# Batch 0 of an attention-and-FFN kernel: blocks of 128, 256 and 384 query rows against two blocks of 384

## Chip, cores and metric

The kernel runs on one core of a Trainium2 chip. The metric is the device time of one execution in microseconds (us). Five engines work beside each other: PE (matmuls; its weight loads are shown as PEld), DVE (elementwise, reads PSUM), ACT (activations, reads PSUM), POOL and SP. SP and POOL also issue DMAs.

## What is computed

```python
# B, H, S, D = 4, 8, 768, 64; 16 centroids a head
q_assign = argmax(q_n @ c_n.T); k_assign = argmax(k_n @ c_n.T)   # per head
mask = q_assign[:, :, :, None] == k_assign[:, :, None, :]
scores = where(mask, q @ k.T / 8, -1e9)
attn = softmax(scores) @ v                       # (B, H, S, D)
x = attn.transpose(0, 2, 1, 3).reshape(3072, 512)
out = (sigmoid(x @ w_gate) * (x @ w_val)) @ w_out   # 512 -> 1536 -> 512
```

Each query sees only the keys that fall to the same centroid. An FFN with a sigmoid gate follows.

## The kernel before

Heads go in pairs (4 pairs a batch), keys in 6 chunks of 128, queries in blocks of n x 128 rows. The work on a pair has two halves.

**Preparing a pair.** q and k are loaded by SP in fp32 (load_side, load_pair, L73 to L84), split into a high and a low fp16 part (split_h L189 on DVE or ACT, split_l L197 on DVE), and transposed: for batches 0 and part of 1 by PE (trans_pe L211, evac L222), later by DMA (trans_dma L230). PE then multiplies with the centroids (logits L237, 24 small matmuls a side), and DVE takes the maximum and compares (onehot L251). The one-hot rows, scaled, become 16 more rows of the transposed q and k, so that the score matmul itself adds a large constant where the clusters agree. They get there in two ways: rows (L274) transposes on PE, copies on DVE and sends them with small DMAs of 24 KB from SP; rows_pad (L292), used for k of batch 0 and q of its pair 0, transposes them padded, so that one copy by DVE or ACT from PSUM puts them in place.

**Attention** (att, L436). For each pair and key chunk: two score matmuls (L490), one exp over both heads on ACT (L499), and, behind it, 2 x n AV matmuls (L450), one exp behind for n = 1 and two for more. At the end of a pair DVE adds the mean term of v and takes the reciprocal (L460, L469), and Pool (DVE for n = 1) multiplies (L470). v is cast by prep_v (L361, one pair at a time, Pool or ACT), and its sum over keys comes from mean_v: for batch 0 by 24 matmuls on the casts, for later batches by Pool's sum_v and a single matmul a half batch.

**FFN** (ffn_in L520, ffn_out L546). 96 matmuls for n x 128 rows with tanh on ACT (L540) and a product on DVE (L542), then 12 matmuls of 512 columns (L552) for each 128 rows. The FFN of one block is cut into single matmuls, which ffn_some hands out between the steps of the next block's attention.

**Batch 0** runs in blocks of 128, 256 and 384 queries, every other batch in two of 384 (BLK, L565). For the first block the rows 0, 6, 12 ... of q are loaded for all heads in one tile (qn0, L93), and have a path of their own (q0_split, q0_trans, q0_classify, q0_rows; T0), so that only k must be prepared in full for it (first_block, L622). The other queries of batch 0 are prepared during the first two blocks. xT, the transposed input of the FFN, comes for the first two blocks from PE transposes (x_trans, L422), else from a DMA transpose (L511).

The order of work is written by hand in the lead-in and from the middle of the third block on. Between, PE, DVE and ACT are left to a scheduler, while SP and POOL keep the program's order; an instruction that depends on nothing can still come to stand earlier than the program has it, among the instructions of the lead-in. at (L573) lists what is to be issued at which half step. Three PSUM banks ("f") serve everything but scores and AV.

Of the kernel before, what the change touches and what calls it, by code (L numbers as in the profile page):

```python
# [20 lines left out]
def kernel(  # L21
# [18 lines left out]
    MCH = 3  # L40
    MB = MCH * 128
    NFC = FF // 128
    NDC = DM // 128
    es_scale = 1.0 / (D ** 0.5 * SC * SC)
# [15 lines left out]
    hp = ctx.enter_context(tc.tile_pool(name="h", bufs=1))  # L60
# [12 lines left out]
    def load_side(b, pr, side):  # L73
        t = NAT[b, pr, side] = natp.tile([128, 2, NCH, D], FP, name="nat")
        nc.sync.dma_start(
            out=t,
            in_=(q, k)[side][b, 2 * pr : 2 * pr + 2].rearrange(
                "h (p c) d -> p h c d", c=NCH
            ),
        )  # L80

    def load_pair(b, pr):
        load_side(b, pr, 1)
        load_side(b, pr, 0)  # L84

    def load_v(b, g):
# [5 lines left out]

    qn0 = natp.tile([128, H, D], FP, name="nat")  # L93
    nc.sync.dma_start(
        out=qn0, in_=q[0].rearrange("h (p c) d -> p h c d", c=NCH)[:, :, 0, :]
    )
    for pr in range(NPR):
        load_side(0, pr, 1)
    load_v(0, 0)
    load_v(0, 1)  # L100
    for pr in range(NPR):
        load_side(0, pr, 0)
# [24 lines left out]
    ohq0 = const.tile([128, H, D + NCL], HP)  # L127
    nc.gpsimd.memset(ohq0, 0.0)
    ohk0 = [const.tile([128, 2, NCH, D + NCL], HP, name=f"ohk0{i}") for i in range(2)]
    nc.gpsimd.memset(ohk0[0], 0.0)  # L130
    nc.gpsimd.memset(ohk0[1], 0.0)
# [119 lines left out]
    def onehot(b, pr, side):  # L251
        if b == 0 and (side == 1 or pr == 0):
            dst = ohk0[pr % 2][:, :, :, D : D + NCL]
        else:
            if side == 1 or b == 0:
                OH[b, pr] = ohp.tile([128, NCH, 2, 2, NCL], HP, name="ohw")
            dst = OH[b, pr][:, :, side, :, :].rearrange("p c h x -> p h c x")
        clv = CL[b, pr, side][:, 0 : 2 * NCH * NCL].rearrange("p (g x) -> p g x", x=NCL)
        mx = smp.tile([128, 2 * NCH], FP, name="mx")
        nc.vector.tensor_reduce(mx, clv, AX.X, ALU.max)  # L260
        nc.vector.tensor_tensor(
            dst,
            clv.rearrange("p (h c) x -> p h c x", h=2),
            mx.rearrange("p (h c) -> p h c", h=2)
            .unsqueeze(3)
            .to_broadcast([128, 2, NCH, NCL]),
            ALU.is_equal,
        )
# [5 lines left out]
    def rows(b, pr):  # L274
        ns = 1 if b == 0 else 2
        po = fp_.tile([32 * ns, 1024], HP, name="f")
        for c in range(NCH):
            nc.tensor.transpose(  # L278
                po[:, bass.ts(c, 128)],
                OH[b, pr][:, c, 0:ns, :, :].rearrange("p s h x -> p (s h x)"),  # L280
                ident,
            )
        ohc = ohp.tile([32 * ns, S], HP, name="ohc")
        nc.vector.tensor_scalar(ohc, po[:, 0:S], OHV, None, ALU.mult)
        for side in range(ns - 1, -1, -1):
# [6 lines left out]
    def rows_pad(pr, side, hh, eng=None):  # L292
        po = fp_.tile([128, 1024], HP, name="f")
        for c in range(NCH):
            nc.tensor.transpose(  # L295
                po[0 : D + NCL, bass.ts(c, 128)], ohk0[pr % 2][:, hh, c, :], ident
            )
        dst = T[0, pr, side][D : D + NCL, hh, :]
# [7 lines left out]
    hl0 = hlp.tile([128, H, 2, D], HP, name="hl")  # L306
    T0 = const.tile([128, H, 128], HP)

    def q0_split():
        nc.vector.tensor_scalar(hl0[:, :, 0, :], qn0, SC, None, ALU.mult)  # L310
        nc.vector.scalar_tensor_tensor(
            hl0[:, :, 1, :], qn0, SC, hl0[:, :, 0, :], ALU.mult, ALU.subtract
        )

    def q0_trans():
        pt = fp_.tile([128, 1024], HP, name="f")
        for h in range(H):
            nc.tensor.transpose(
                pt[:, bass.ts(h, 128)], hl0[:, h, :, :].rearrange("p a d -> p (a d)"), ident
            )  # L320
        nc.scalar.copy(T0.rearrange("p h n -> p (h n)"), pt)

    def q0_classify():
        cl = fp_.tile([128, 512], FP, name="f")
        for h in range(H):
            for r in range(2):
                nc.tensor.matmul(
                    out=cl[:, bass.ts(h, NCL)],
                    lhsT=T0[:, h, :],
                    rhs=cT[:, r, bass.ts(h, NCL)],  # L330
                    start=(r == 0),
                    stop=(r == 1),
                )
        clv = cl[:, 0 : H * NCL].rearrange("p (h x) -> p h x", x=NCL)
        mx = smp.tile([128, 2 * NCH], FP, name="mx")
        nc.vector.tensor_reduce(mx[:, 0:H], clv, AX.X, ALU.max)
        nc.vector.tensor_tensor(
            ohq0[:, :, D : D + NCL],
            clv,
            mx[:, 0:H].unsqueeze(2).to_broadcast([128, H, NCL]),  # L340
            ALU.is_equal,
        )

    def q0_rows():
        po = fp_.tile([128, 1024], HP, name="f")
        for h in range(H):
            nc.tensor.transpose(po[0 : D + NCL, bass.ts(h, 128)], ohq0[:, h, :], ident)
        nc.vector.tensor_scalar(
            T0[D : D + NCL, :, :].rearrange("p h n -> p (h n)"),
            po[D : D + NCL, :],  # L350
            OHV,
            None,
            ALU.mult,
        )


# [4 lines left out]
    def prep_v(b, pr, eng=None):  # L361

        va = VA[b, pr] = vap.tile([128, 2, NCH, D + 1], HP, name="va", bufs=2 * NPR)
        nc.gpsimd.memset(va[:, :, :, D : D + 1], 1.0)
        h = 2 * (pr % 2)
        src = VN[b, pr // 2][:, h : h + 2, :, :]
        if eng is nc.scalar:
            nc.scalar.copy(va[:, :, :, 0:D], src)
        else:
            nc.gpsimd.tensor_copy(va[:, :, :, 0:D], src)  # L370

    def sum_v(b, g):
        hs = bass.ts(g, H // 2)
        vn = VN[b, g]
        if g == 0:
            VS[b] = smp.tile([128, H, D + 1], HP, name="vs", bufs=1)
            nc.gpsimd.memset(VS[b][:, :, D : D + 1], float(NCH))
# [9 lines left out]
    def mean_v(b, hs):  # L387

        if b not in SV:
            SV[b] = vap.tile([128, H, D + 1], FP, name="sv")  # L390
        sp = fp_.tile([128, 512], FP, name="f")
        n = len(hs) * (D + 1)
        if b == 0:
            for c in range(NCH):
                nc.tensor.matmul(
                    out=sp[:, 0:n],
                    lhsT=ones,
                    rhs=VA[b, hs[0] // 2][:, :, c, :],
                    start=(c == 0),
                    stop=(c == NCH - 1),  # L400
                )
        else:
            nc.tensor.matmul(
                out=sp[:, 0:n],
                lhsT=ones,
                rhs=VS[b][:, hs[0] : hs[-1] + 1, :],
                start=True,
                stop=True,
            )
        nc.vector.tensor_scalar(  # L410
            SV[b][:, hs[0] : hs[-1] + 1, :].rearrange("p h d -> p (h d)"),
            sp[:, 0:n],
            EPS,
            None,
            ALU.mult,
# [3 lines left out]
    X = {}  # L419
    XT = {}  # L420

    def x_trans(b, c0, n, pr):  # L422

        if pr == 0:
            XT[b, c0] = xp.tile([128, MCH, NDC, 128], HP, name="xT")
        ps = fp_.tile([128, 1024], HP, name="f")
        for t in range(n):
            nc.tensor.transpose(
                ps[:, bass.ts(t, 128)], X[b, c0][:, t, bass.ts(pr, 128)], ident
            )  # L430
        nc.vector.tensor_copy(
            XT[b, c0][:, 0:n, pr, :],
            ps[:, 0 : n * 128].rearrange("p (t n) -> p t n", t=n),
        )

    def att(b, c0, n):  # L436
        x = X[b, c0] = xp.tile([128, MCH, DM], HP, name="x")
        pend = []
        G = 3 if n == 1 else 1
        avt = [None]  # L440

        def av_part(pr, j0, es):
            if j0 == 0:
                avt[0] = avp.tile([128, 512], FP, name="av")
            av = avt[0]
            for g in range(G):
                for hh in range(2):
                    for t in range(n):
                        o = (hh * n + t) * (D + 1)
                        nc.tensor.matmul(  # L450
                            out=av[:, o : o + D + 1],
                            lhsT=es[:, hh, bass.ts(g * n + t, 128)],
                            rhs=VA[b, pr][:, hh, j0 + g, :],
                            start=(j0 + g == 0 and hh == 0 and t == 0),
                            stop=(j0 + g == NCH - 1 and hh == 1 and t == n - 1),
                            skip_group_check=True,
                        )
            if j0 + G == NCH:
                s = smp.tile([128, 2, MCH, D + 1], FP, name="avs")
                nc.vector.tensor_tensor(  # L460
                    s[:, :, 0:n, :],
                    av[:, 0 : 2 * n * (D + 1)].rearrange("p (h t d) -> p h t d", h=2, t=n),
                    SV[b][:, 2 * pr : 2 * pr + 2, :]
                    .unsqueeze(2)
                    .to_broadcast([128, 2, n, D + 1]),
# [334 lines left out]
```

## Time and profile before

| | us |
|---|---|
| median of 3 runs (364.88 to 366.35) | 365.16 |
| the profiled execution | 365.16 |
| its span in the profile | 363.4 |
| first scores of batch 0, of its block of 256, of 384 | 15.1, 33.8, 62.2 |
| first scores of batch 1, 2, 3 | 91.9, 172.9, 255.2 |

The first scores are the first start of line L490 for each block; two score matmuls start at 15.1, and the ten that follow at 16.4. In the page, a group's line gives busy time and mean ns of one; "idle before" is the engine's idle time and what ended it. PEclk is the clock granted to PE. A view of busy times by stretch has the stretch, its length, then busy us and number of instructions of PE, PEld, DVE, ACT and POOL, the granted clock, the share of busy DMA engines and GB/s. A view in order of time has start, duration, engine, line, operation, out<-in and count, and in brackets the idle time before and what ended it.

### The profile page before, as it was taken

To read this page: it belongs to the slowest core of one execution; us is meant where nothing else is said; L and a number is where in the kernel's file an instruction comes from. 1 tells how busy PE (TensorE), PEld (TensorE's weight loads), DVE (VectorE), ACT (ScalarE), POOL (GpSimd) and SP (SyncE) were. 2 spreads that over 40 slices of the span, in tenths; PEclk is the share of its full clock that TensorE was granted. 3 is DMA by queue.
4 is the path that set the end of the run, shared out by engine and by line. 5 is a ranking of instruction groups with operands and counts; after the bars stand their busy time and mean duration, and the time that the engine had idled before them with its cause. 6 is when DMAs were issued, how large, how long until landed. Compare 5 with 4: busy or idle time off the path is not lost.

```text
span 363.4 us, 9364 instructions
## 1 busy us (share of the span) xinstructions
PE 344.6 (95%) x3887; PEld 228.1 (63%) x3887; DVE 169.5 (47%) x374; ACT 244.6 (67%) x359; POOL 71.5 (20%) x105
## 2 busy tenths in 40 slices
PE   8699999999989999989999999989999999999995
PEld 4597877876566656656556656656556656664652
DVE  4678686647164725373344725373313322331330
ACT  6687698686577575857577574857578867881421
POOL 3720021436010120425010120425000000000000
PEclk9989999999999999999999999999999999999999
DMA  8999279466629363760619373761310031003002
GB/s 258 338 203 191 66 223 185 128 142 89 154 95 248 71 168 89 200 160 12 164 67 261 30 199 86 236 112 27 73 74 2 0 74 58 2 2 101 32 0 87
DMA packets 67466, 42.72 MB, mean 118 GB/s; under 512 B 45568, under 2 KB 64352, under 8 KB 67424
## 3 DMA queue, kind: packets, MB, share of 16 engines
q1 hardware_dynamic: 61488, 37.38, 40.0%
q0 software_dynamic: 5792, 4.72, 8.3%
q8 instruction: 30, 0.49, 0.5%
q14 instruction: 12, 0.10, 0.1%
q10 hardware_dynamic: 144, 0.03, 0.0%
HBM read 28.61 MB, written 6.29 MB: 96 GB/s over the span
## 4 chain that ended last, share of the span: by engine, by line
PE 78%; DMA 6%; DVE 5%; issue 5%; ACT 4%; SPq 1%; POOL 0%; ACTq 0%; DVEq 0%
PE f L531 30%; PE f L552 16%; PE sc L490 15%; PE av L450 8%; PE f L243 4%; DMA vn<-in_v_dram 3%; ACT es L499 2%; PE f L216 2%; DVE hl L195 1%; DMA out_dram<-osb 1%; PE f L278 1%; DVE hT L542 1%; DMA nat<-in_q_dram 1%; DMA nat<-in_k_dram 1%; PE f L295 1%
## 5 line engine op out<-in xcount | busy, mean ns | idle before, releaser
L499 ACT ACTIVATE es<-sc,nbias 128x768 f16<-128x768 f32 (+1 forms) x200 | 173.6, 877 | 71.1 <-PE sc L490 66.2
L542 DVE SCALAR_TENSOR_TENSOR hT<-g,f 128x384 f16<-128x384 f32 (+1 forms) x96 | 51.1, 534 | 84.0 <-PE f L531 46.4
L450 PEld LDWEIGHTS <-es 128*128 128x128 f16 x1152 | 59.8, 97 | 27.1 <-issue 3.7
L470 POOL TENSOR_TENSOR x<-avs,ri 128x384 f16<-128x384 f32 (+1 forms) x32 | 26.8, 837 | 245.5 <-DVE ri L469 196.6
L450 PE MATMUL av<-va,es 128*128 128x65 f16 x1152 | 67.5, 194 | 1.3 <-DVE avs L460 0.7
L540 ACT ACTIVATE g<-f 128x384 f32<-128x384 f32 (+2 forms) x108 | 48.8, 452 | 18.6 <-PE f L531 9.7
L552 PE MATMUL f<-wo_194,hT 128*128 128x512 f16 x138 | 38.3, 379 | 0.0
L552 PE MATMUL f<-wo_193,hT 128*128 128x512 f16 x138 | 38.1, 379 | 0.0
L460 DVE TENSOR_TENSOR avs<-av,sv 128x390 f32<-128x390 f32 (+2 forms) x36 | 18.6, 516 | 41.0 <-PE av L450 40.4
L552 PEld LDWEIGHTS <-hT 128*128 128x128 f16 x276 | 24.4, 97 | 21.1
L200 DVE SCALAR_TENSOR_TENSOR hl<-nat,hl 128x768 f16<-128x768 f32 x32 | 32.6, 1017 | 0.8
L260 DVE TENSOR_REDUCE mx<-f 128x12 f32<-128x192 f32 x32 | 11.4, 356 | 32.3 <-PE f L243 32.2
L561 ACT ACTIVATE osb<-f 128x512 f32<-128x512 f32 x24 | 14.2, 593 | 17.6 <-PE f L552 15.3
L531 PE MATMUL f<-xT,w_186 128*128 128x384 f16 (+2 forms) x108 | 25.6, 308 | 0.0
L531 PE MATMUL f<-xT,w_187 128*128 128x384 f16 (+2 forms) x108 | 25.6, 307 | 0.0
L531 PE MATMUL f<-xT,w_188 128*128 128x384 f16 (+2 forms) x108 | 24.1, 307 | 0.4 <-DVE hT L542 0.4
L531 PE MATMUL f<-xT,w_191 128*128 128x384 f16 (+2 forms) x108 | 24.0, 307 | 0.5 <-ACT g L540 0.5
L531 PE MATMUL f<-xT,w_189 128*128 128x384 f16 (+2 forms) x108 | 23.8, 307 | 0.5 <-DVE hT L542 0.5
L531 PE MATMUL f<-xT,w_192 128*128 128x384 f16 (+2 forms) x108 | 23.6, 307 | 0.4 <-DVE hT L542 0.4
L531 PE MATMUL f<-xT,w_190 128*128 128x384 f16 (+2 forms) x108 | 23.8, 307 | 0.0
L531 PE MATMUL f<-xT,w_185 128*128 128x384 f16 (+2 forms) x108 | 23.6, 308 | 0.2
L370 POOL CAST va<-vn 128x768 f16<-128x768 f32 x15 | 14.2, 951 | 10.6 <-DMA vn<-in_v_dram 10.6
(221 smaller groups left out, 449.1 us busy)
## 6 DMA issues: line engine op xcount, KB each, us to landing
nat<-in_k_dram SPq DMA_DIRECT2D x16, 384.0 KB, 3.9
vn<-in_v_dram SPq DMA_DIRECT2D x8, 768.0 KB, 6.8
nat<-in_q_dram SPq DMA_DIRECT2D x16, 384.0 KB, 4.8
out_dram<-osb SPq DMA_DIRECT2D x24, 256.0 KB, 2.1
wo_193<-in_moe_w_out_dram POOLq DMA_DIRECT2D x1, 768.0 KB, 17.1
wo_194<-in_moe_w_out_dram POOLq DMA_DIRECT2D x1, 768.0 KB, 12.2
w_185<-in_moe_w_gate_dram POOLq DMA_DIRECT2D x1, 384.0 KB, 7.8
w_189<-in_moe_w_val_dram POOLq DMA_DIRECT2D x1, 384.0 KB, 8.0
```

The source lines that it names most:

```text
L200: nc.vector.scalar_tensor_tensor(hl[:, :, 1, :], nat, SC, hl[:, :, 0, :], ALU.mult, ALU.subtract)
L243: nc.tensor.matmul(out=cl[:, o : o + NCL], lhsT=T[b, pr, side][:, hh, bass.ts(c, 128)], rhs=cT[:, r, bass.ts(2 * pr + hh, NCL)], start=(r ...
L370: nc.gpsimd.tensor_copy(va[:, :, :, 0:D], src)
L450: nc.tensor.matmul(out=av[:, o : o + D + 1], lhsT=es[:, hh, bass.ts(g * n + t, 128)], rhs=VA[b, pr][:, hh, j0 + g, :], start=(j0 + g == 0 ...
L460: nc.vector.tensor_tensor(s[:, :, 0:n, :], av[:, 0 : 2 * n * (D + 1)].rearrange("p (h t d) -> p h t d", h=2, t=n), SV[b][:, 2 * pr : 2 * p ...
L470: (nc.vector if n == 1 else nc.gpsimd).tensor_tensor(x[:, 0:n, 2 * pr * D : 2 * (pr + 1) * D].rearrange("p t (h d) -> p h t d", h=2), s[:, ...
L490: nc.tensor.matmul(out=sc[:, hh, g * n * 128 : (g + 1) * n * 128], lhsT=T[b, pr, 1][0 : D + NCL, hh, bass.ts(j0 + g, 128)], rhs=rhs, start ...
L499: nc.scalar.activation(es[:, :, 0:w], sc[:, :, 0:w], AF.Exp, bias=nbias, scale=es_scale)
L531: nc.tensor.matmul(out=gv[i][:, 0:w], lhsT=wgv[i][fc * NQ // NFC][:, dc, bass.ts(fc % (NFC // NQ), 128)], rhs=xT[:, 0:n, dc, :], start=(dc ...
L540: nc.scalar.activation(g[:, 0:w], gv[0][:, 0:w], AF.Tanh, scale=0.5)
L542: nc.vector.scalar_tensor_tensor(hT[:, fc, 0:w], g[:, 0:w], 1.0, gv[1][:, 0:w], ALU.add, ALU.mult)
L552: nc.tensor.matmul(out=o, lhsT=hT[:, fc, bass.ts(t, 128)], rhs=wo[fc * 2 // NFC][:, fc % (NFC // 2), :], start=(fc == 0), stop=(fc == NFC ...
```

## The change

Batch 0 runs in two blocks of 384, as the other batches do. BLK, T0 and its functions, rows_pad for other pairs than the first, x_trans, and the split of the FFN into two generators go. The lead-in prepares pair 0 in full (q and k) and part of pair 1; the rest of batch 0 is prepared in its first block through at and by_pe, with rows for pairs 1 to 3. SP loads pair 0, pair 1, half of v, pairs 2 and 3, the other half. v is cast half a batch at a time on Pool, and its sum over keys comes for batch 0 too from sum_v on Pool and one matmul a half. Weights come in quarters during batch 0, at steps 0.5 to 20.5, w_out at 26 and 31. From the lead-in to the end of the first block PE, DVE and ACT are ordered by the scheduler; the second block is ordered by hand. hT has two buffers.

```diff
-    qn0 = natp.tile([128, H, D], FP, name="nat")
-    nc.sync.dma_start(
-        out=qn0, in_=q[0].rearrange("h (p c) d -> p h c d", c=NCH)[:, :, 0, :]
-    )
-    for pr in range(NPR):
-        load_side(0, pr, 1)
+    load_pair(0, 0)
+    load_pair(0, 1)
     load_v(0, 0)
+    load_pair(0, 2)
+    load_pair(0, 3)
     load_v(0, 1)
-    for pr in range(NPR):
-        load_side(0, pr, 0)
...
-    hp = ctx.enter_context(tc.tile_pool(name="h", bufs=1))
+    hp = ctx.enter_context(tc.tile_pool(name="h", bufs=2))
...
-    def rows_pad(pr, side, hh, eng=None):
+    def rows_first(side, hh, eng=None):
         po = fp_.tile([128, 1024], HP, name="f")
         for c in range(NCH):
             nc.tensor.transpose(
-                po[0 : D + NCL, bass.ts(c, 128)], ohk0[pr % 2][:, hh, c, :], ident
+                po[0 : D + NCL, bass.ts(c, 128)], oh0[:, side, hh, c, :], ident
             )
...
-    def prep_v(b, pr, eng=None):
+    def prep_v(b, g):
+        hs = bass.ts(g, H // 2)
+        vn = VN[b, g]
+        if g == 0:
+            VA[b] = vap.tile([128, H, NCH, D + 1], HP, name="va")
...
+        nc.gpsimd.tensor_copy(VA[b][:, hs, :, 0:D], vn)
...
-        if b == 0:
-            for c in range(NCH):
-                nc.tensor.matmul(
...
+        nc.tensor.matmul(out=sp[:, 0:n], lhsT=ones, rhs=VS[b][:, hs, :], start=True, stop=True)
...
-    BLK = [[(0, 1), (1, 2), (3, 3)]] + [[(0, 3), (3, 3)]] * (B - 1)
...
+    def lead_in():
+        split(0, 0, 1)
+        split_h(0, 0, 0, nc.scalar)
+        split_l(0, 0, 0)
+        for hh in range(2):
+            trans_pe(0, 0, 1, hh)
+            evac(0, 0, 1, hh)
         finish_centroids()
+        warm(1)
+        trans_pe(0, 0, 0, 0)
+        evac(0, 0, 0, 0, nc.scalar)
+        trans_pe(0, 0, 0, 1)
+        evac(0, 0, 0, 1, nc.scalar)
+        split(0, 1, 1)
+        warm(2)
         logits(0, 0, 1)
+        onehot(0, 0, 1, oh0[:, 1, :, :, D : D + NCL])
+        warm(2)
+        logits(0, 0, 0)
+        onehot(0, 0, 0, oh0[:, 0, :, :, D : D + NCL])
+        split_h(0, 1, 0, nc.scalar)
         prep_v(0, 0)
+        rows_first(1, 0)
+        rows_first(1, 1)
+        warm(2)
+        rows_first(0, 0, nc.scalar)
+        rows_first(0, 1)
+        trans_pe(0, 1, 1, 0)
+        evac(0, 1, 1, 0)
+        trans_pe(0, 1, 1, 1)
+        evac(0, 1, 1, 1)
+        split_l(0, 1, 0)
+        warm(2)
...
+    at(0, 1.5, classify, 0, 1, 1)
+    at(0, 2.5, classify, 0, 1, 0)
+    at(0, 3.5, rows, 0, 1)
+    by_pe(0, 2, (2, 3, 4, 5, 6, 7, 8.5))
+    by_pe(0, 3, (8, 9, 10, 11, 12, 13, 14))
+    for n, step in enumerate((0.5, 5, 12, 19)):
+        at(0, step, load_w, 0, n)
+        at(0, step + 1.5, load_w, 1, n)
+    at(0, 26, load_wo, 0)
+    at(0, 31, load_wo, 1)
+    at(0, 2, sum_v, 0, 0)
+    at(0, 3, prep_v, 0, 1)
+    at(0, 4, sum_v, 0, 1)
+    at(0, 5.5, mean_v, 0, 0)
+    at(0, 10.5, mean_v, 0, 1)
+    at(0, 10, load_pair, 1, 0)
+    at(0, 17, load_pair, 1, 1)
+    by_pe(1, 0, (22, 23, 24, 25, 26.5, 28, 29))
+    by_pe(1, 1, (27, 28, 29, 30, 31.5, 33, 34))
...
+    lead_in()
+    first.close()
+    first.enter_context(tc.manual_schedule(engines={mybir.EngineType.SP, mybir.EngineType.Pool}))
+    LAG = 5
+    prev = None
     for b in range(B):
+        for qb in range(NQB):
+            if b == 0 and qb == 1:
+                first.close()
+                ctx.enter_context(tc.manual_schedule())
+            for half, _ in enumerate(att(b, qb)):
+                if half == 2 * (LAG if b == 0 else LAG + 2) and prev is not None:
+                    fq.append(ffn(*prev))
+                if half < 2 * NST:
+                    for fn, args in plan.get((b, 2 * qb * NST + half), ()):
+                        fn(*args)
+                ffn_some(132.0 / (2 * NST + 1))
+            prev = (b, qb)
```

## The prediction

> **What bounds the kernel now.** I read the page first, then the busy times by stage, then the order of time around the start.
>
> ```profile
> span 363.4 us, 9364 instructions
> ## 1 busy us (share of the span) xinstructions
> PE 344.6 (95%) x3887; PEld 228.1 (63%) x3887; DVE 169.5 (47%) x374; ACT 244.6 (67%) x359; POOL 71.5 (20%) x105
> ```
>
> PE is busy 95%, so the time falls only with less PE work or less PE waiting. Where that could be is shown by the stages (us; busy time and instructions of PE, PEld, DVE, ACT, POOL; granted clock; DMA):
>
> ```profile
> 0.00:16.40 16.40, 11.41 (x134) 7.05 (x134) 8.98 (x24) 9.67 (x14) 8.46 (x21) 1.00 0.93 307
> 16.40:33.50 17.10, 15.88 (x285) 14.58 (x286) 14.74 (x39) 14.44 (x18) 4.37 (x7) 0.90 1.31 205
> 33.50:62.00 28.50, 26.87 (x473) 22.52 (x471) 20.66 (x56) 22.93 (x44) 3.91 (x5) 1.00 0.64 162
> 62.00:91.90 29.90, 28.95 (x411) 22.66 (x409) 18.04 (x42) 21.01 (x33) 13.21 (x18) 1.00 0.59 114
> 91.90:172.90 81.00, 77.67 (x879) 49.84 (x878) 39.03 (x80) 55.65 (x78) 17.11 (x23) 1.00 0.54 134
> ```
>
> The edges are the first scores of batch 0 (16.4), its block of 256 (33.5), of 384 (62.0) and batch 1 (91.9). From 91.9 on both kernels run the same blocks of 384, so the change is decided by when batch 1 begins.
>
> Busy time includes each matmul's drain, so I count PE work by start-to-start: 96 L531 matmuls of 384 columns took 15.60 us and 36 L552 took 7.77 at the end of the chain, so 0.162 and 0.216; 12 transposes 0.67, 24 logits 0.59, an AV 0.029. By that the PE holds 73.7 us of work before 91.9, and 18.2 of waits.
>
> **The work.** The built order of the changed kernel, at these rates: lead-in 9.4; block 0 20.0 (48 scores 7.8, 138 AVs 4.0, 78 transposes 4.4, 144 logits 3.6, 2 sums 0.2); block 1 37.1 (scores 7.8, 150 AVs 4.4, 96+9 FFN matmuls 17.5, 144 logits 3.6, 66 transposes 3.7, 0.1). In all 66.5: 7.2 less, mostly rows_pad, mean_v of batch 0, x_trans and the T0 path. From batch 1 on it is 255 in both, except that the first FFN is 27 output matmuls short at the border instead of 24: 3 x 0.216 = +0.6. So the change wins unless PE waits over 25 us before batch 1. It has no FFN to run in block 0; I therefore follow the chain.
>
> **Lead-in.** Times are on this trace's clock. The rows I use:
>
> ```profile
> 11.14 1.07 POOL L370 CAST va<-vn 128x768 f16<-128x768 f32 x1 [7.40 <-DMA vn<-in_v_dram]
> 12.16 0.94 POOL L169 DMA_DIRECT2D w_185<-in_moe_w_gate_dram  x1
> 17.23 1.69 ACT L499 ACTIVATE es<-sc,nbias 128x768 f16<-128x768 f32 x2
> 84.35 1.04 POOL L470 TENSOR_TENSOR x<-avs,ri 128x384 f16<-128x384 f32 x1 [3.58 <-DVE ri L469]
> 84.74 1.46 DVE L200 SCALAR_TENSOR_TENSOR hl<-nat,hl 128x768 f16<-128x768 f32 x1
> 85.38 1.51 POOL L370 CAST va<-vn 128x768 f16<-128x768 f32 x1
> ```
>
> The scheduler puts pair 2's split ahead of pair 0's one-hots in DVE's queue: split_h k2, max k0, split_l k2, one-hot k0, max q0, split_l q2, one-hot q0. DVE therefore waits for the sixth and seventh load. v, whose end Pool awaited at 11.1, came after 2.62 MB; k2 comes after 2.75 MB, so 11.5 at 382 GB/s (window 6.9 to 10.3). The first gate quarter is now issued by POOL at about 1 us: the eight quarters landed 1.94 us apart (12.16+7.8 for the first, 19.15+14.4 for the last). It delays k2 by 0 to 1.9; I take 1.9, as the quarters run at full rate beside nothing else: k2 13.4, q2 14.5. The seven DVE steps follow each other at 0.47, 0.27, 0.87, 0.28, 0.27, 0.87, 0.28 (rows L195 0.55, L260 and L261 0.36, L200 0.95, each less the 0.08 by which the next one starts early): 16.8.
>
> Pool now casts and sums v just then (cast of 1536 about 1.7, sums 1.81+0.73+0.73, twice, against three casts before). The rows at 84.7 show what that costs: a split_l of 0.95 took 1.46 when it met x, and the cast behind it 1.51 instead of 0.83. I charge 0.5 here (bounds 0 to 1.8, one Pool sum): 17.3. The Trainium skill (SBUF — State Buffer, Who interferes with whom) has it that a VectorE operation with two SBUF inputs and a GpSimd one that reads SBUF exclude each other for a whole instruction. The trace agrees (1.46 for 0.95); by that rule alone the sum would be up to 1.3 higher. The next steps go by the rows again.
>
> Two row copies (0.55 each) and a third, whose transposes await the first one's bank, end at 19.4. PE then has been mostly idle and is slow:
>
> ```profile
> 13.70:17.20 3.50, 1.69 (x41) 1.54 (x41) 1.49 (x3) 3.45 (x5) 3.50 (x8) 0.99 1.13 324
> 17.20:20.60 3.40, 3.40 (x44) 3.40 (x42) 2.27 (x4) 3.13 (x5) 3.05 (x5) 0.50 1.31 204
> ```
>
> After a stretch with PE busy 1.69 of 3.50 us the clock was 0.50 for the next 3.4. The idle here is longer, so six transposes (0.65) and two warm-up matmuls (0.43 each, L111's cold rate) precede the scores: first scores 20.5 instead of 16.4, first exp 21.0.
>
> **Block 0** is ACT's: two exps take 1.69, so 0.85 each against 0.5 of PE. Exps 0 to 5 with a copy and a split (0.8 each): 27.7. Pair 1's rows no longer come by copies from PSUM (rows_pad) but through rows(): behind 5.6 us of DVE (two evacuations, split_l q1, split k3, split_l q3, two one-hots), which waits for ACT's half of the q3 split at 24.3 and so ends at 26.0, 0.7 for a second meeting with Pool, 0.5 for six transposes and 0.55 for the copy: 27.8, Then come four DMAs on SP's queue, 0.6 apart and 1.85 to land, 31.5: first exp of pair 1 at 31.9, a new wait of 4.2 on ACT, and PE and DVE, which have pair 2 to prepare, cannot use all of it. Pair 2's rows land in time. 12 exps, a copy and a split: 43.7. Pair 3's rows stand behind batch 1's split (1.35) on DVE: 2.2 more, 45.9. Six exps: 51.0.
>
> **Block 1.** FFN starts when x is transposed: avs 0.57, reciprocal 0.19, x 0.85, xT 3.7 and the last AV, 5.5; but its PSUM bank hangs on the row copy of batch 1, 1.5 more: 58.0. Left are 37.1 - 6.4 = 30.7 of PE work and 2.4 of waits (62.0 to 91.9: 29.9 less 27.6 of work): batch 1 at 91.1.
>
> **What the trace of before does not show.** Row DMAs among the weight loads: alone 1.8 to 1.9, slowest row 4.1 (T_3280<-ohc), so 0 to 2.2 at each of two waits; 0.8 in all, nearer to the usual rows. The clock after pair 3's wait: 0 to 1.7 (half of one 3.4 us stretch), I take 1.0, as the row above has lost the clock with half its stretch busy. The Trainium skill (TensorE: Matmul & The Clock Gate, Part 1) asks for a whole idle window of 3.4 us; 1.69 busy of 3.50 contradicts it, and by the page the sum would be 1.0 lower. Hand-overs between engines: 0 to 1.5 (PE lost 4.6 in 16.4 to 33.5 in small ones), 0.5. I cost at nothing: the second hT buffer (from 328 on PE runs 36, 96 and 36 matmuls with one buffer and no gap), v in one tile instead of one a pair (Pool writes it a half-batch ahead), and xT by DMA for block 0 beyond its 3.7 (hidden behind the scores of block 1; bare, it is the 5.5 above). Batch 1 at 91.1 + 2.3 = 93.4.
>
> **Sum.** 93.4 - 91.9 + 0.6 = +2.1. The profiled execution took 365.16, 1.76 over its span, and the median of the three runs is the same: 367.3.
>
> **Rivals.**
> - *The waits eat just the saving* (no change): the first quarter of weights moves behind the loads, which gives back 1.9: 365.4. For it: in before a quarter took 7.8 from issue to landing. Against: 16 engines carry both.
> - *Less PE work wins* (faster): DVE passes pair 1's rows out before exp 5 ends. The price is the wait of 4.2, of which 1 stays, and 1.9 of weights and the clock's 1.0 with it: 367.3 - 3.2 - 1.9 - 1.0 = 361.2. It decides where k2 lands by 11.5 and the rows' four DMAs start before 25. Against: PE, ACT and DVE all wait on one DVE queue.
> - *The clock falls through block 0* (much slower): PE has 20.0 of work in 30 us; each stretch below half costs up to 1.7; three more give 372.4. For it: 1.69 of 3.50 was enough. Against: 26.87 of 28.50 kept it.
> - *Weights are not behind batch 0*: the built order has the first quarter as POOL's second instruction and both halves of w_out before the second quarter. All land before FFN starts (8 x 1.94 + 2 x 3.8 = 23 from 17), so this costs only the lead-in, counted above.
>
> **Chances.** 0.5% is 1.8 us, about what a measurement of this kernel can tell from no change. Forecast (367.0 to 370) 0.40, clock (370 and over) 0.15, no change (363.3 to 367.0) 0.27, faster 0.18. Summed bounds: weights 1.9, lock 1.2, clock 1.0 and row DMAs 0.8 absent give 362.4; both row waits at their 2.2 (+3.6), the clock's 1.7 (+0.7) and more lock (+0.8) give 372.4. The range 362.4 to 372.4 leaves out about 0.2; the likeliest case alone is 367.0 to 370.
>
> **What would show it.** First scores at 20 to 21, with DVE idle before a split_h until a load lands; about 4 us without exp before pair 1; a granted clock of 0.5 around 17 to 21; batch 1 beginning at 92 to 95; from there the same 271.5. I am wrong if the first scores come before 18 or if batch 1's own stages change length.

## The result and the profile after

The changed kernel took 380.85 us (median of 4 runs, 378.70 to 382.46) against 365.42 of the kernel before beside it: a ratio of 1.0416, with a 95% interval of 1.0356 to 1.0476. The forecast had the direction, not the size: +2.1 us was said and +15.4 came. The profiled execution took 380.14.

The page of the changed kernel: PE is busy about as long (346.7 us against 344.6), but for a smaller share of the span.

```profile
span 378.4 us, 8785 instructions
## 1 busy us (share of the span) xinstructions
PE 346.7 (92%) x3650; PEld 219.6 (58%) x3650; DVE 168.0 (44%) x335; ACT 236.7 (63%) x331; POOL 77.3 (20%) x91
...
PEclk9779875999999999999999999998999999999999
```

The busy times by stage, with edges at the first scores (24.9), pair 1 (37.05), about the end of block 0's scores (61.9) and batch 1 (104.3):

```profile
0.00:24.90 24.90, 15.52 (x133) 9.60 (x134) 15.49 (x29) 8.18 (x11) 15.06 (x23) 0.79 1.01 272
24.90:37.05 12.15, 9.30 (x189) 7.64 (x188) 9.51 (x21) 7.09 (x9) 2.73 (x4) 1.00 1.02 169
37.05:61.90 24.85, 17.69 (x212) 11.69 (x212) 8.54 (x17) 15.55 (x19) 4.94 (x7) 0.72 0.79 168
61.90:104.30 42.40, 40.52 (x526) 28.37 (x525) 26.32 (x53) 29.02 (x41) 13.70 (x14) 0.96 0.47 90
104.30:185.60 81.30, 78.11 (x881) 50.02 (x880) 39.74 (x79) 55.85 (x78) 17.11 (x18) 1.00 0.57 134
```

The first three rows hold most of the loss. In the third PE is busy 17.69 of 24.85 us and the granted clock is 0.72. What PE waited for up to 105 us (in total, times, longest):

```profile
PE f L283 <- DVE oh_142 L250: 7.8, 2, 7.1
PE sc L382 <- DMA T_724<-ohc: 5.1, 1, 5.1
PE f L266 <- DVE ohw L250: 1.4, 2, 0.8
PE sc L382 <- ACT es L390: 1.3, 3, 0.7
PE sc L382 <- DMA T_364<-ohc: 1.2, 1, 1.2
```

Two waits stand out: 7.1 in the lead-in for pair 0's one-hots, and 5.1 for the DMAs that bring pair 3's one-hot rows. ACT, which needs pair 3's scores, stood idle for 6.75 before them:

```profile
57.37 1.69 ACT L390 ACTIVATE es<-sc,nbias 128x768 f16<-128x768 f32 x2 [6.75 <-PE sc L382]
```

In the kernel before, such a row DMA of batch 0 looked like this in the list of DMA issues (KB each, median us from issue to landing):

```profile
T_761<-ohc SPq DMA_DIRECT2D x2, 24.0 KB, 1.9
```

In the changed kernel's list, between 30 and 62 us, the rows of pairs 1 (T_335, T_364) and 3 (T_689, T_724) take 1.7 to 2.9 times as long:

```profile
w_181<-in_moe_w_gate_dram POOLq DMA_DIRECT2D x1, 384.0 KB, 5.0
w_185<-in_moe_w_val_dram POOLq DMA_DIRECT2D x1, 384.0 KB, 4.9
w_182<-in_moe_w_gate_dram POOLq DMA_DIRECT2D x1, 384.0 KB, 6.6
...
T_335<-ohc SPq DMA_DIRECT2D x2, 24.0 KB, 4.5
T_364<-ohc SPq DMA_DIRECT2D x2, 24.0 KB, 3.3
...
T_689<-ohc SPq DMA_DIRECT2D x2, 24.0 KB, 5.5
T_724<-ohc SPq DMA_DIRECT2D x2, 24.0 KB, 5.0
```

The lead-in on DVE and on POOL, in order of time:

```profile
14.41 0.84 DVE L186 TENSOR_SCALAR hl<-nat 128x768 f16<-128x768 f32 x1 [3.71 <-DMA nat<-in_k_dram]
15.17 0.34 DVE L249 TENSOR_REDUCE mx<-f 128x12 f32<-128x192 f32 x1
15.44 2.78 DVE L191 SCALAR_TENSOR_TENSOR hl<-nat,hl 128x768 f16<-128x768 f32 x1
18.14 0.35 DVE L250 TENSOR_TENSOR oh_142<-f,mx 128x192 f16<-128x192 f32 x1
```

```profile
15.58 1.81 POOL L312 TENSOR_TENSOR nat<-vn 128x768 f32<-128x768 f32 x1
```

As forecast, DVE waits for pair 2's k (14.4) before it may write pair 0's one-hots. The split behind it takes 2.78 where it takes 0.95 alone: it meets Pool's sum of v, and the excess (1.83) is the length of that one Pool instruction (1.81).

From batch 1 on, where both kernels were said to be alike, 273.2 us follow its first exp, against 270.9 before. The loss of 15 us thus has several places, and I tried each.

### The profile page after: what moved, and what is told of

Read it like the earlier page. It is cut to its first block, busy times and chain, and to the rows that moved or that the text cites. A ratio compares the mean times of both kernels' runs of the same rounds, so it can differ in the third digit from the quotient of the medians.

```text
span 378.4 us, 8785 instructions
## 1 busy us (share of the span) xinstructions
PE 346.7 (92%) x3650; PEld 219.6 (58%) x3650; DVE 168.0 (44%) x335; ACT 236.7 (63%) x331; POOL 77.3 (20%) x91
## 4 chain that ended last, share of the span: by engine, by line
PE 81%; DVE 6%; DMA 5%; issue 4%; ACT 2%; SPq 1%; DVEq 0%; ACTq 0%
PE f L416 31%; PE f L434 17%; PE sc L382 16%; PE av L347 8%; PE f L234 4%; DMA nat<-in_k_dram 3%; PE f L207 2%; DVE hl L186 2%; PE f L266 1%; DMA T_724<-ohc 1%; DMA T_364<-ohc 1%; DVE hT L427 1%; DVE hl L191 1%; DVE mx L249 1%; ACT es L390 1%
## 5 line engine op out<-in xcount | busy, mean ns | idle before, releaser
L390 ACT ACTIVATE es<-sc,nbias 128x768 f16<-128x768 f32 x192 | 171.6, 902 | 82.9 <-PE sc L382 78.7
L427 DVE SCALAR_TENSOR_TENSOR hT<-g,f 128x384 f16<-128x384 f32 x96 | 52.8, 551 | 83.8 <-PE f L416 50.3
L369 POOL TENSOR_TENSOR x<-avs,ri 128x384 f16<-128x384 f32 x32 | 27.3, 852 | 251.1 <-DVE ri L368 212.0
L425 ACT ACTIVATE g<-f 128x384 f32<-128x384 f32 x96 | 46.7, 486 | 23.7 <-PE f L416 14.0
L357 DVE TENSOR_TENSOR avs<-av,sv 128x390 f32<-128x390 f32 x32 | 18.0, 563 | 53.8 <-PE av L347 53.2
L434 PE MATMUL f<-wo_188,hT 128*128 128x512 f16 x144 | 40.4, 379 | 0.0
L434 PE MATMUL f<-wo_187,hT 128*128 128x512 f16 x144 | 39.9, 379 | 0.0
L434 PEld LDWEIGHTS <-hT 128*128 128x128 f16 x288 | 25.4, 97 | 21.6
L191 DVE SCALAR_TENSOR_TENSOR hl<-nat,hl 128x768 f16<-128x768 f32 x32 | 34.5, 1081 | 1.3 <-ACT hl L184 0.4
L416 PE MATMUL f<-xT,w_181 128*128 128x384 f16 x96 | 25.5, 332 | 0.0
L416 PE MATMUL f<-xT,w_180 128*128 128x384 f16 x96 | 25.2, 326 | 0.0
L249 DVE TENSOR_REDUCE mx<-f 128x12 f32<-128x192 f32 x32 | 11.3, 354 | 31.1 <-PE f L234 31.1
L443 ACT ACTIVATE osb<-f 128x512 f32<-128x512 f32 x24 | 14.2, 594 | 15.8 <-PE f L434 15.5
L416 PE MATMUL f<-xT,w_185 128*128 128x384 f16 x96 | 23.6, 333 | 0.5 <-ACT g L425 0.5
L416 PE MATMUL f<-xT,w_179 128*128 128x384 f16 x96 | 23.3, 325 | 0.8 <-DVE T_1203 L219 0.3
L416 PE MATMUL f<-xT,w_182 128*128 128x384 f16 x96 | 22.9, 325 | 0.9 <-DVE hT L427 0.9
L416 PE MATMUL f<-xT,w_183 128*128 128x384 f16 x96 | 22.9, 325 | 0.5 <-DVE hT L427 0.5
L416 PE MATMUL f<-xT,w_184 128*128 128x384 f16 x96 | 22.9, 325 | 0.0
L416 PE MATMUL f<-xT,w_186 128*128 128x384 f16 x96 | 22.8, 325 | 0.0
L186 DVE TENSOR_SCALAR hl<-nat 128x768 f16<-128x768 f32 x26 | 16.2, 622 | 4.2 <-DMA nat<-in_k_dram 4.2
## 6 DMA issues: line engine op xcount, KB each, us to landing
wo_188<-in_moe_w_out_dram POOLq DMA_DIRECT2D x1, 768.0 KB, 13.4
```

What stands on the lines that cost most here:

```text
L186: nc.vector.tensor_scalar(hl[:, :, 0, :], nat, SC, None, ALU.mult)
L191: nc.vector.scalar_tensor_tensor(hl[:, :, 1, :], nat, SC, hl[:, :, 0, :], ALU.mult, ALU.subtract)
L357: nc.vector.tensor_tensor(s, av[:, 0 : 2 * QCH * (D + 1)].rearrange("p (h t d) -> p h t d", h=2, t=QCH), SV[b][:, 2 * pr : 2 * pr + 2, :] ...
L369: nc.gpsimd.tensor_tensor(x[:, :, 2 * pr * D : 2 * (pr + 1) * D].rearrange("p t (h d) -> p h t d", h=2), s[:, :, :, 0:D], ri.unsqueeze(3). ...
L390: nc.scalar.activation(es, sc[:, :, 0:QB], AF.Exp, bias=nbias, scale=es_scale)
L416: nc.tensor.matmul(out=gv[i][:, 0:QB], lhsT=wgv[i][fc * NQ // NFC][:, dc, bass.ts(fc % (NFC // NQ), 128)], rhs=xT[:, :, dc, :], start=(dc ...
```

## The experiments

**Theory 1**: the weight quarters in flight hold up the small row DMAs of pairs 1 and 3. **Theory 2**: the lead-in, that is DVE's order and Pool's sums beside DVE. **Theory 3**: the throttled clock is a cost of its own. The table gives each kernel's median and, from its profiled execution, where the time lies: the first exp, then the lengths from first exp to first exp.

| kernel | median us | first exp | pair 0 | pair 1 | pair 2 | pair 3 | block 1 | batches 1 to 3 |
|---|---|---|---|---|---|---|---|---|
| changed | 380.85 | 25.4 | 12.9 | 6.6 | 12.4 | 6.1 | 41.7 | 273.2 |
| few_weights | 373.88 | 23.1 | 12.3 | 6.7 | 9.0 | 6.1 | 41.8 | 273.4 |
| rows_by_copies | 370.99 | 23.6 | 10.3 | 7.3 | 6.9 | 6.0 | 41.8 | 273.3 |
| copies_few | 370.01 | 24.8 | 9.7 | 7.3 | 6.9 | 4.9 | 40.9 | 273.1 |
| hand_order | 382.01 | 16.4 | 18.6 | 11.8 | 12.9 | 6.6 | 43.1 | 271.6 |
| mean_on_pe | 377.03 | 22.7 | 13.5 | 6.9 | 11.9 | 5.6 | 42.2 | 273.6 |
| warm_lead | 379.64 | 24.6 | 12.0 | 7.2 | 12.4 | 5.7 | 42.2 | 273.6 |
| w0_late | 379.51 | 23.0 | 14.4 | 7.3 | 12.4 | 5.9 | 40.8 | 272.9 |
| split_cast | 377.98 | 25.7 | 14.2 | 7.2 | 12.4 | 5.8 | 40.8 | 270.6 |
| copies_mean | 368.68 | 24.3 | 9.7 | 8.0 | 6.9 | 4.9 | 40.9 | 275.2 |
| copies_mean_hand | 369.36 | 16.2 | 12.6 | 11.0 | 9.4 | 5.4 | 41.2 | 271.7 |
| copies_mean_split | 366.00 | 23.3 | 9.7 | 8.0 | 6.9 | 4.9 | 40.9 | 270.3 |
| lead_hand | 362.52 | 16.4 | 11.4 | 9.8 | 6.8 | 6.1 | 41.7 | 270.7 |

A pair's length includes the wait for the next pair's rows. Kernels with the same lead-in differ by some 2 us in the first exp (23.1, 23.6, 25.4, 25.7), in step with the landing of pair 2's k, for which DVE waits (12.9, 12.9, 14.4, 15.0). So a difference of 2 us between the first exps of two profiles shows no effect of an edit.

### The weights, and the row DMAs

few_weights:

```diff
-    wgv = [[wp.tile([128, NDC, FQ], HP, name=f"w{i}{n}") for n in range(NQ)] for i in range(2)]
-    wo = [wp.tile([128, NFC // 2, DM], HP, name=f"wo{n}") for n in range(2)]
+    w1 = wp.tile([128, NDC, FQ], HP, name="w00")
+    wgv = [[w1] * NQ for i in range(2)]
+    wo = [wp.tile([128, NFC // 2, DM], HP, name="wo0")] * 2
...
```

> Leaves out seven of the eight weight quarters and one half of w_out: one quarter and one half are loaded and stand for all, so the output is not the reference's; every instruction of PE, ACT and DVE stays. In the changed kernel the row DMAs of pairs 1 and 3 took about 5 us from issue to landing beside the weight loads, first exp of pair 1 at 38.4, first scores of pair 3 at 56.2, batch 1 at 104.3, 380.9 us in all. Theory 1 (weight loads hold up the small row DMAs): they land 1.9 after issue, pair 1's first exp at 35.5, pair 3's scores by 52, less throttled time after them, batch 1 at 95 to 99, 372 to 376 us. Theory 2 (the lead-in's order and lock): nothing moves after the lead-in, batch 1 at 103 to 105, 379 to 382.

Measured 373.88 us (371.26 to 374.44), ratio to the kernel before 1.0184 (1.0116 to 1.0252): 7.0 less than the changed kernel. In its list of DMA issues up to 62 us the median of the twelve row DMAs is 1.9 again:

```profile
T<-ohc SPq DMA_DIRECT2D x12, 24.0 KB, 1.9
```

The eight of pairs 1 and 3 took 1.8 to 1.9 each. Pair 2's four took 2.1 to 3.4 with no weights in flight, so something else can slow them too. The table says where the gain lies: of 6.1 us in the profiled executions 3.4 are ahead of pair 3 (12.4 to 9.0), 0.6 ahead of pair 1 and 2.3 ahead of the first exp. The last part is not shown to be the weights': until pair 2's k landed, only the first quarter was in flight in both kernels. Theory 1 holds, above all at pair 3.

rows_by_copies brings batch 0's other rows as pair 0's are brought:

```diff
     def rows(b, pr):
+        if b == 0:
+            for side in (1, 0):
+                for hh in range(2):
+                    rows_first(side, hh, nc.scalar if hh else None, pr)
+            return
...
-        onehot(b, pr, side)
+        onehot(b, pr, side, oh0[:, side, :, :, D : D + NCL] if b == 0 else None)
```

> Batch 0's pairs 1 to 3 take their one-hot rows from PSUM by padded transposes and four copies of 0.55 (half on ACT), as the kernel before did, in place of a copy and four DMAs; weights load as in the changed kernel. Theory 1: no wait for row DMAs is left; 72 more transposes (4.0 us of PE) and 9 more copies cost less than the two waits of 3 and more and the throttled time behind them: batch 1 at 97 to 100, 373 to 377 us. Theory 2: the lead-in is the same (first scores at 25), the copies cost ACT and DVE what the DMAs did: 380 to 384.

Measured 370.99 (370.39 to 371.56), ratio 1.0126 (1.0079 to 1.0173): 9.9 less, and more than I had expected (1.8 of its profile's 9.1 lie ahead of the first exp). None of PE's larger waits before batch 1 is for a row DMA any more; pair 0 is 2.6 and pair 2 5.5 us shorter. The DMAs cost even without weights beside them: few_weights against this, 2.0 ahead of pair 1 and 2.1 ahead of pair 3, for four DMAs issued 0.6 apart and 1.9 each. The expectation counted 72 further transposes; they are 54, since 18 go, and they and the 9 further copies lie beside other work.

copies_few has both edits.

> Rows of pairs 1 to 3 by copies, as in rows_by_copies (371.0 us), and in addition seven of the eight weight quarters and one half of w_out left out as in few_weights (373.9 us), so the output is not the reference's. If the weight loads cost block 0 only through the row DMAs: nothing left to gain, 370 to 372. If they also hold up the loads of batch 0's and batch 1's inputs or SBUF's other users: 367 to 369.

Measured 370.01 (367.74 to 371.30), ratio 1.0124 (1.0073 to 1.0175). With the row DMAs gone, leaving out the weights gains nothing that can be told apart: they acted through the row DMAs.

### The lead-in

hand_order:

```diff
-    first.enter_context(tc.manual_schedule(engines={mybir.EngineType.SP, mybir.EngineType.Pool}))
+    first.enter_context(tc.manual_schedule())
```

> All engines of block 0 run in the order in which the program writes the instructions, in place of the scheduler's order for PE, DVE and ACT. Pair 2's splits then stand behind pair 0's one-hots. Theory 2 (lead-in): first scores at 20 to 21 in place of 24.9, no 2.78 us split ahead of the one-hots, and the 4 us stay to the end: 375 to 378. Theory 1: the lead-in gains, but pair 1's rows wait for the weight quarters in flight all the same (landing at 36 to 37) and pair 3's too: batch 1 at 102 to 104, 379 to 381.

Measured 382.01 (381.85 to 382.82), ratio 1.0431 (1.0383 to 1.0479). Both expectations were too low. The first exp comes 9.0 us earlier than in the changed kernel, and nothing of it reaches the end: pair 0 is 5.7 and pair 1 5.2 longer. The edit fixes the order of all of block 0, so it doesn't show what the order of the lead-in costs by itself; an earlier lead-in alone is not enough. The other half of theory 2, Pool beside DVE, shows in this kernel's DVE and POOL, in order of time:

```profile
20.11 3.36 DVE L186 TENSOR_SCALAR hl<-nat 128x768 f16<-128x768 f32 x1
```

```profile
19.81 1.47 POOL L306 CAST va<-vn 128x1536 f16<-128x1536 f32 x1
21.24 1.80 POOL L312 TENSOR_TENSOR nat<-vn 128x768 f32<-128x768 f32 x1
```

A split of 0.55 took 3.36: it began beside the cast and ended 0.4 after the sum behind it had ended. The Trainium skill (SBUF — State Buffer, Who interferes with whom) calls this an exclusive lock, and the trace agrees; here one DVE instruction was held through two Pool instructions.

mean_on_pe:

```diff
-        nc.tensor.matmul(out=sp[:, 0:n], lhsT=ones, rhs=VS[b][:, hs, :], start=True, stop=True)
+        for c in range(NCH if b == 0 else 1):
+            nc.tensor.matmul(
+                out=sp[:, 0:n],
+                lhsT=ones,
+                rhs=VA[b][:, hs, c, :] if b == 0 else VS[b][:, hs, :],
+                start=(c == 0),
+                stop=(b > 0 or c == NCH - 1),
+            )
...
-    at(0, 2, sum_v, 0, 0)
...
-    at(0, 4, sum_v, 0, 1)
```

> Batch 0's sums of v are left to PE (six matmuls a half over the fp16 v, as the kernel before did) and the two sum_v on Pool go. Theory 2 (Pool's sum locks DVE): the split that took 2.78 takes 0.95 again, first scores at 23.1, one-hots 1.8 earlier, 377 to 379 us. Theory 1: Pool comes to the weight loads 3 us earlier per half, so the quarters crowd the row DMAs as before or more: 379 to 382.

Measured 377.03 (375.99 to 378.19), ratio 1.0291 (1.0237 to 1.0346): 3.8 less. The split that took 2.78 takes 0.94:

```profile
13.12 0.85 DVE L186 TENSOR_SCALAR hl<-nat 128x768 f16<-128x768 f32 x1 [2.69 <-DMA nat<-in_k_dram]
13.89 0.34 DVE L249 TENSOR_REDUCE mx<-f 128x12 f32<-128x192 f32 x1
14.15 0.94 DVE L191 SCALAR_TENSOR_TENSOR hl<-nat,hl 128x768 f16<-128x768 f32 x1
```

That is 1.8 of the 3.8; the rest isn't accounted for (this profile's lead-in also began with its inputs 1.3 earlier).

w0_late issues the first two quarters and w_out behind the cast of v, and nothing ahead of the inputs:

```diff
         prep_v(0, 0)
+        load_w(0, 0)
+        load_w(1, 0)
+        for n in range(2):
+            load_wo(n)
...
```

> The changed kernel with no weights ahead of batch 0's inputs: the first quarter, which Pool issued at 1.3 us, and the three loads that the scheduler would put in its place (second quarter, both halves of w_out) are issued behind the cast of v. Forecast's rival (the first quarter of 1.9 us delays k2 and with it the one-hots): k2 lands at 12 to 13 in place of 14.4, first scores 1.9 earlier, 378 to 380 us. If the lead-in is hidden behind pair 1's row DMAs, which now have more weights beside them: 380 to 383.

Measured 379.51 (378.48 to 380.22), ratio 1.0381 (1.0343 to 1.0419). k2 landed at 11.3 in place of 14.4, and the first scores came at 22.5. Of the 3.1 us some 1.3 are left, and the two kernels' runs overlap: inconclusive between the two expectations. In the lead-in a part was lost again, as two of DVE's splits took 2.31 and 2.55 (2.78 and 1.10 in the changed kernel). My rival "faster" was to decide where k2 lands by 11.5 and pair 1's row DMAs start before 25; k2 did, the DMAs started at 29.8.

### The clock

warm_lead puts `warm(24)` ahead of pair 0's row transposes.

> The changed kernel with 24 more warm-up matmuls (of 0.22 us at full clock) ahead of pair 0's row transposes, where PE stood idle for 7.15 us. Theory 3 (the throttled clock is a cost of its own): the clock stays full past 14, the six transposes and the matmuls before the first scores come 1 to 2 us earlier, 378 to 380. If the clock in the lead-in is hidden behind the row DMAs of pair 1: no change, 380 to 382.

Measured 379.64 (379.30 to 380.67), ratio 1.0389 (1.0357 to 1.0421). The clock stayed at 1.0 up to 20.2 in place of 14.0, and the gain of 1.2 is again inside the spread of the changed kernel: inconclusive. The clock's price shows better elsewhere in the table: pair 3 took 6.0 and block 1 41.8 in rows_by_copies, at half clock from 49.4 to 56.2, and 4.9 and 40.9 in the three kernels whose clock stayed full there (copies_few, copies_mean, copies_mean_split). The difference of 2.0 is what two such stretches of 3.4 cost here.

### Together, and the batches behind

copies_mean is rows_by_copies with mean_on_pe.

> Both of the edits that helped together: rows of pairs 1 to 3 by copies from PSUM, and batch 0's sums of v by PE. Alone they gave 371.0 and 377.0 us against 380.9 of the changed kernel (-9.9 and -3.8). If the row DMAs (theory 1) and Pool's sums beside DVE (theory 2) are separate costs they add: 366.5 to 368.5. If both only fed the same wait before pair 1, 370 to 371.

Measured 368.68 (368.51 to 371.69), ratio 1.0101 (1.0057 to 1.0145). 2.3 more is gained, less than the sum. In the table it lies in pair 3 and block 1, so in the full clock. That this edit keeps the clock there is not shown: copies_few kept it with Pool's sums in place. The profiled execution is the slowest of the four, and batches 1 to 3 lost two stretches of full clock in it (275.2).

copies_mean_hand adds hand_order's edit.

> The same two edits and block 0 in the program's order. Hand order alone brought the first scores from 24.9 to 15.9 but pair 1's first exp only from 38.4 to 35.0, and the time to 382.0. Theory 1 (the rows' DMAs took the lead back): without them the lead lasts: batch 1 at 89 to 93, 360 to 365 us. Theory 2b (the lead is lost because block 0's own preparation of pairs, on DVE, ACT and PE in one fixed order, is the limit): pair 1's first exp stays near 31 to 33, block 1 begins at 54 or later, 367 us and over.

Measured 369.36 (368.06 to 370.09), ratio 1.0096 (1.0066 to 1.0127). Theory 2b was right on the time and on block 1, if not on pair 1, which came at 28.8 and not at 31 to 33: the first exp comes 8.1 earlier than in copies_mean, and block 1 begins no earlier. In a fixed order pairs 0, 1 and 2 take 2.9, 3.0 and 2.5 longer.

copies_mean_split lets Pool cast v for batches 1 to 3 in halves; split_cast does so in the changed kernel alone:

```diff
...
-        at(b - 1, 32 if b == 1 else 22, prep_v, b, 0)
+        for i in range(2):
+            at(b - 1, (32 if b == 1 else 22) + i, prep_v, b, 0, i)
+            at(b - 1, 43 + i, prep_v, b, 1, i)
...
-        at(b - 1, 43, prep_v, b, 1)
```

> The two edits, and for batches 1 to 3 Pool casts v in halves of 768 a pair (0.83 us) as before, in place of 1536 at once (1.5 to 1.7). From batch 1 on the changed kernel took 2.6 us more than the kernel before, with a split on DVE of 1.40 for 0.55 and a throttled stretch behind it near 253. If the longer cast is the cause: 2 to 2.6 less than copies_mean. If it is the border's extra FFN matmuls (0.6 predicted) or the clock's phase, at most 0.6 less.

Measured 366.00 (365.13 to 367.55, 10 runs), ratio 1.0005 (0.9981 to 1.0028): 2.7 less.

> The changed kernel with only Pool's cast of v in halves of 768 for batches 1 to 3. Beside the two other edits it took 2.7 us off. If the long cast's hold on DVE's split is the cause, and not the clock's phase that those edits set: 377.8 to 379, and 271.5 to 272.5 from batch 1 on in place of 274.1. If it was the phase: 380 to 382.

Measured 377.98 (376.76 to 378.66), ratio 1.0329 (1.0295 to 1.0363): 2.9 less. Batches 1 to 3 take 270.3 and 270.6, as before (270.9). In the changed kernel this is how the cast of 1536 at once tells, on DVE and POOL in order of time, and in the busy times behind it:

```profile
253.33 1.40 DVE L186 TENSOR_SCALAR hl<-nat 128x768 f16<-128x768 f32 x1
255.64 0.54 DVE L272 TENSOR_SCALAR ohc<-f 64x768 f16<-64x768 f16 x1
```

```profile
252.85 1.47 POOL L306 CAST va<-vn 128x1536 f16<-128x1536 f32 x1 [1.69 <-DMA vn<-in_v_dram]
```

```profile
252.90:256.30 3.40, 1.47 (x12) 0.80 (x12) 3.37 (x6) 1.42 (x3) 1.42 (x1) 1.00 0.60 116
256.30:259.70 3.40, 3.40 (x17) 1.87 (x18) 0.74 (x2) 1.01 (x2) 0.00 (x0) 0.51 0.67 130
```

The split is held 0.85 longer, PE waits 1.4 us for the row copy L272 behind it, which holds a PSUM bank, PE is busy 1.47 of 3.40, and the next 3.4 us run at half clock. In split_cast the cast takes 0.82, the same split 1.11, and with PE busy 1.92 of the same stretch of 3.4 the clock stays full:

```profile
252.60:256.00 3.40, 1.92 (x19) 1.16 (x17) 3.37 (x5) 1.90 (x3) 0.82 (x1) 1.00 0.48 99
256.00:259.40 3.40, 3.05 (x29) 2.03 (x30) 1.65 (x4) 1.63 (x4) 0.00 (x0) 1.00 0.79 152
```

The clock is the larger part of this cost by the profiled executions. The three kernels with the casts in halves lost no stretch of full clock in batches 1 to 3 (270.3 to 270.7). Of the ten with the whole cast eight lost one or two (272.9 to 275.2), and the two in a fixed order, hand_order and copies_mean_hand, lost none and took 271.6 and 271.7.

lead_hand is copies_mean_split with the program's order up to step 4 of block 0, and the scheduler's behind it.

```diff
...
+                if (b, qb, half) == (0, 0, 8):
+                    first.close()
+                    first.enter_context(
+                        tc.manual_schedule(
+                            engines={mybir.EngineType.SP, mybir.EngineType.Pool}
+                        )
+                    )
```

> The three edits that helped (rows by copies, batch 0's sums on PE, casts in halves: 366.0 us) and the program's order up to step 4 of block 0 only, the scheduler's behind it, so that pair 2's splits no longer stand ahead of pair 0's one-hots. The whole block in hand order gave first scores at 15.6 but block 1 at 54.6, against 23.7 and 53.8. If the splits ahead of the one-hots cost time to the end: first scores at 16, pair 1's first exp at 28 to 29, block 1 at 48 to 50, 361 to 364 us, under the kernel before (365.4). If block 0's preparation of pairs 2 and 3 (DVE, PE and the DMA of q3 and k3) is the limit and not the lead-in: block 1 at 52 to 54, 365 to 368.

Measured 362.52 (361.25 to 364.73, 6 runs), ratio 0.9916 (0.9884 to 0.9948): 0.8% faster than the kernel before. Its PE is busy 95%, as before the change, with 173 matmuls fewer:

```profile
span 362.8 us, 8903 instructions
## 1 busy us (share of the span) xinstructions
PE 343.7 (95%) x3714; PEld 220.7 (61%) x3714; DVE 166.9 (46%) x338; ACT 241.5 (67%) x337; POOL 70.8 (20%) x91
```

So the two blocks of 384 are worth having, together with what came with them (the second hT buffer, v in one tile, the place of the weights), which was not tried apart. With the row waits gone the lead-in counts, though of 6.9 us by the first exp 3.5 remain: pairs 0 and 1 are 3.5 longer, and in its profiled execution, the slowest of its six, half clock from 45.3 to 52.1 takes 2 more.

## Why the prediction was wrong

**The step that failed** is the first of the unknown costs, "Row DMAs among the weight loads: alone 1.8 to 1.9, slowest row 4.1 [...], so 0 to 2.2 at each of two waits; 0.8 in all, nearer to the usual rows". The mechanism was named; the term was mis-sized. Leaving out the weights gave 7.0 us in the medians, of which the profiled executions show 4.0 at the two waits. At pair 3 the rows needed 6.7 from the end of the copy (49.5) to the last landing (56.2), and 3.8 in few_weights, so 2.9 where 2.2 was the bound; at pair 1 they needed 5.3 from the first issue to the last landing, and 3.8 there. The usual rows of before were no guide: none of them had weight quarters in flight. The range held neither this nor the others together.

This step is not the only miss. Step by step, the profiled execution (380.14) took 12.8 more than the forecast: 4.4 up to the first exp, 2.0 in pair 0, 5.0 in pairs 1 and 2, 2.0 in pair 3 and block 1, and 1.7 in batches 1 to 3, less the 2.3 that the sum held for the unknown costs.

Point by point:

- **PE work** in block 0 and block 1, said to be 20.0 and 37.1: 19.7 and 37.3 by the same count. In the lead-in PE stands idle, so its work there decides nothing. With the waits undone the two blocks of 384 took 362.5, so there is a saving; how much of it is PE's work was not measured apart.
- **Lead-in 20.5**: its mechanism stood as said (DVE waits for k2, then for Pool), its size did not: 24.9. k2 landed at 14.4 (said 13.4), and the lock cost 1.83 at one split (0.5 taken, 0 to 1.8 as bounds, chosen at the wrong end). Some 1.7 more came behind the one-hots, where PE ran at half clock and the third row copy ended at 23.7 (said 19.4). To carry the lead-in's whole delay into the sum is not borne out: w0_late has the first exp 2.4 earlier and is no faster that can be told apart, nor is hand_order with 9.0, though that one also orders the rest of block 0.
- **Pair 1 at 31.9**: 38.4. The wait on ACT is there, 5.15 in place of 4.2, so most of the miss is the late start (4.4):

```profile
38.36 1.69 ACT L390 ACTIVATE es<-sc,nbias 128x768 f16<-128x768 f32 x2 [5.15 <-PE sc L382]
```

- **Pair 3 with a wait of 2.2**: 6.75 on ACT (its row stands with the result), the largest miss of a wait. This wait was attributed to the row copy behind batch 1's split on DVE; the DMAs behind that copy ended it.
- **Clock 1.0**: half clock from 51.6 to 65.2 in the changed kernel, for which pair 3 and block 1 bear 2.0 by the table. The rival "the clock falls through block 0" was nearer than the forecast, but its price of 1.7 a stretch lay on top of waits that I had too small.
- **"From 91.9 on both kernels run the same blocks"**: wrong by 2.3 in the profile and 2.9 by split_cast. I had priced the cast of 1536 in the lead-in and not in batches 1 to 3, where it is there too.
- **Weights not behind batch 0 "costs only the lead-in"**: wrong, since they were in flight when the row DMAs were issued.
- **FFN start 58.0**: 71.8, from the same waits, and xT took 5.2 from issue to landing (3.7 taken). The 27 output matmuls carried over, +0.6: not to be seen (270.6 in split_cast).
- **Where the block of 384 began**: the table of the kernel before gives 62.2 for its first scores, but they start at 56.4; 62.2 is the last of its first pair's. The prediction's edge of 62.0 therefore lies inside that block. Its forecast took from that edge only the 2.4 of waits up to 91.9 (29.9 less 27.6 is 2.3), so little hangs on it.
- **Second hT buffer, one tile for v**: not tried alone.

The parts, one after the other in medians: rows by copies -9.9, sums on PE -2.3, casts in halves -2.7, lead-in order -3.5; 380.9 to 362.5.

## What to carry to other kernels

A small DMA that a matmul waits for must not be priced at its quiet-time latency when bulk loads are in flight: look at which queues are busy when it is issued, or bring the data over PSUM. A wait that a change shortens counts only if nothing behind it waits for something else: undo it alone, and then again with the other waits gone. Here a lead-in in the program's order gained 3.5 once the other waits were gone and the scheduler had the rest of the block (lead_hand); with the whole block in that order it gained nothing, with the waits (hand_order, +1.2) or without (copies_mean_hand, +0.7). A longer instruction on POOL can be a longer hold on DVE in any stage, so price it in every stage, not only where the change is about.

## What was not expected of the hardware

- **Row DMAs of 24 KB beside weight loads.** Pair 3's four landed at 54.9, 55.8, 56.0 and 56.2, 4.8 to 5.7 us after their issue; the quarter w_182 landed at 55.6, and w_181 and w_185 had taken 4.9 to 5.0. The small DMAs took as long as the bulk ones. The DMA packets by queue (number, MB, their time as a share of the 16 engines'; q0 carries POOL's weights, q1 what SP issues) show how, first from 49.5, when the first row was issued, to 53.5, then from 53.5 to 56.3:

```profile
q0 software_dynamic: 753, 0.57, 110.6%
q1 hardware_dynamic: 452, 0.57, 66.6%
q0 software_dynamic: 303, 0.22, 51.7%
```

For 4 us after the issue not one packet of SP's queue ran. In few_weights the first one came 1.1 after the issue (46.7). The Trainium skill (DMA: Bandwidth & Descriptors, Queues, rings and completion order) has each DMA engine take turns between the queues packet by packet; by that alone I should expect a share of the rate and not a quarter's whole length. At pair 1 the trace has such a sharing (109 packets of SP's queue beside 677 of the weights' from 31.9 to 35.9), at pair 3 it has not. What decides between the two stays open.
- **The clock was lost with more than half a stretch busy, and came back late.** Around pair 3, by stretches:

```profile
48.10:51.50 3.40, 2.01 (x32) 1.29 (x28) 2.65 (x4) 2.52 (x4) 1.64 (x3) 1.00 0.57 58
51.50:54.90 3.40, 0.00 (x0) 0.00 (x0) 0.39 (x2) 0.00 (x0) 1.57 (x2) 0.51 1.28 212
54.90:58.40 3.50, 1.52 (x5) 0.65 (x6) 0.00 (x0) 1.03 (x2) 0.00 (x0) 0.50 1.13 311
58.40:61.80 3.40, 3.40 (x26) 2.06 (x26) 0.00 (x0) 3.11 (x4) 0.00 (x0) 0.50 1.00 256
61.80:65.20 3.40, 3.40 (x35) 2.87 (x34) 1.01 (x3) 2.06 (x3) 0.00 (x0) 0.50 0.00 0
```

2.01 of 3.40 busy lost it here, and 1.92 of 3.40 kept it in split_cast, which is too close to tell. In mean_on_pe the first of these two stretches, with 2.79 busy, was followed by one at 0.50, and the second, with 1.78 busy, by one at 1.00:

```profile
63.20:66.60 3.40, 2.79 (x69) 2.04 (x65) 2.76 (x7) 3.40 (x5) 0.02 (x1) 1.00 0.73 103
169.00:172.40 3.40, 1.78 (x15) 0.89 (x16) 3.37 (x7) 0.90 (x1) 0.00 (x0) 1.00 0.60 113
```

So the busy time of one stretch, as the profile counts it, doesn't decide it alone. In the changed kernel it was still 0.50 after one full stretch (58.4 to 61.8); after 34.4 to 37.9 (1.43 busy) a single full stretch, 37.9 to 41.3, was enough. The Trainium skill (TensorE: Matmul & The Clock Gate, Part 1) has it fall after an idle window and return after one busy window; these rows agree with the window's length of about 3.4 us and with neither condition everywhere.
